# First weights, first residual block and three constants loaded by GpSimd's queue, the second half planned anew, and constant matmuls in TensorE's planned gaps

## The chip, the cores and the metric

The kernel runs on one core of one Trainium2 chip. The core has five instruction streams of its own: TensorE (PE in the profile; its weight loads are PEld), VectorE (DVE), ScalarE (ACT), GpSimd (POOL) and SyncE (SP). Transfers between main memory and the core's SBUF are issued by an instruction of SP, ACT or POOL and carried out by 16 DMA engines beside the compute. The metric is device time of one execution in microseconds (us); lower is better. A comparison gives the median of several executions.

## The reference

Two residual steps over 2048 tokens of 448 channels, each scaled and shifted by rows made of one conditioning vector `c`. The first step is a long convolution along the tokens whose kernel is generated from complex parameters; the second is a gated feed-forward layer with 1792 hidden channels. Everything is float32.

```python
mod = (silu(c) @ w_mod).reshape(1, 6, 1, 448)
sa, ca, ga, sb, cb, gb = (mod[:, i] for i in range(6))
h = layernorm(x) * (1 + ca) + sa
x = x + ga * A(h)
h = layernorm(x) * (1 + cb) + sb
x = x + gb * B(h)

def A(u):                                   # D = 448, N = 256, L = 2048
    K = einsum("dn,dnl,dn->dl", C, exp(dt * A_ * arange(L)), dt * B_).real
    return irfft(rfft(pad(u)) * rfft(pad(K)))[:L] + u * Dskip

def B(x):
    return (gelu(x @ w_gate) * (x @ w_up)) @ w_down
```

## The kernel before

**Two halves.** The first half (to about 400 us of the profile) normalizes the input, generates the convolution kernel and convolves. Six rows of `w_mod` are multiplied with `silu(c)` on TensorE (`mod_row`, task `m.mm`, the multiplications at L768); three of them are needed first, since they scale the first normalization (`norm`, L822 and L823). The normalized input goes through a small transform on TensorE (`ua`, L832) and is stored for later. In parallel the parameters are prepared on VectorE and ScalarE (`prep`), stored, and read back as `lt`; from `lt` come exponentials (`x.mm`, `y.mm`, L593 and L612) and angles (L630) on TensorE, which ScalarE evaluates, VectorE multiplies (L679 to L687) and TensorE contracts (`kgen`, L710). Transforms and products (`k_fft`, then `t_fft` for the last 128 channels: forward L1069, products L1075 and L1078 on VectorE, inverse L1085 on TensorE, eviction `t.z`, store `t.st` L1093) end the half.

**The junction.** The convolution's result is stored to main memory and read back as `yi` (`yi.e` for the first 320 channels; `yi.l0`, `yi.l1` and the short `yi.d..` for the last 128, issued by SP, POOL and ACT, L1154 and L1166). `conv_out(0)` multiplies `yi` with a constant `ai` (L1246 for columns 0 to 320, L1251 for the rest), adds it to the first block of the input, `x1` (L1257), takes the statistics (L1258, L1260, L1274), normalizes (`co.n`, L1288 and L1289), transposes on TensorE with the constant `ident` (`co.t`, L1294 and L1296) and splits the result into two float16 halves `ht` (`co.h` on either engine, `co.l` L1304 on VectorE). For its first two token groups (j = 0, 1) the product is done in two parts, `e` for columns 0 to 320 and `l` for the rest.

**The second half** is the feed-forward layer over four token blocks, the first of them in two halves of 256 tokens for its first four feature groups: `gate_up` (L1365, L1371) and the down product (L1441 for block 0, L1472 after it). Its float32 weights are loaded in pieces of 512 KB (`weight`, L1187, tile `w`, three buffers), split into two float16 parts `wr` (ScalarE L1195, VectorE L1199 and L1200) and stored to main memory for the later blocks.

**What sets the order.** `Plan` holds every piece of work as a `Task` with an engine (or a choice of two), an assumed duration, a due value `v`, and what it depends on. `Plan.order` places the tasks one after the other in the time that it assumes; the due values are shifted by the tables `LEAD` and `LEAN`, numbers per kind of task. What comes out is a fixed list for each engine, which runs in order; real waits are semaphores. SP's list holds nearly all transfers. A transfer takes one of eight completion semaphores in turn, so an issue can also wait for the transfer eight places back. `Plan.run` calls the tasks' functions in the planned order; the tables are long and their numbers tell a reader nothing.

Constants are loaded by `sp`, whose default queue is SP:

```python
def sp(n, v, dst, src, kb, deps=(), alloc=(), use=(), q="SP"):
    qf = adma if q == "ACT" else dma
    return add(n, {q: 0.42 if q == "SP" else 0.1}, v, lambda: qf(dst(), src()), deps, alloc, use, kb=kb)
```

Of the kernel before, what the change touches and what calls it, by code (L numbers as in the profile page):

```python
# [41 lines left out]
    "c.ai": (71.008,), "c.ak": (31.634,), "c.au": (64.741,), "c.ea": (129.571,), "c.id": (-5.74,), "c.ih": (81.5,),  # L42
    "c.ld": (-70.212,), "c.rd": (36.588,), "co.add": (126.534,), "co.adde": (-479.654,), "co.addl": (177.332,),
    "co.addx": (510.429, 276.254, 263.838, 306.027), "co.c2": (-16.462, 185.363, 68.605, 81.504),
    "co.h": (1287.071, 1321.404), "co.h2": (-57.238, -19.565, -34.416, 62.618), "co.l": (166.825, 99.971),
    "co.l2": (-304.102, -376.884, -381.167, -327.959), "co.mm": (1047.13,), "co.mme": (35.95,),
    "co.mml": (321.391,), "co.mmx": (504.891, 504.282, 510.751, 509.801), "co.n": (-32.018, -300.752),
    "co.nx": (-309.183, -245.328, -200.245, -90.738), "co.rc": (52.991, 384.121), "co.rcx": (915.491,),
    "co.rt": (-12.141, 45.958), "co.rtx": (-618.711,), "co.t": (505.324, 339.683),
    "co.t2": (-464.884, -636.939, -578.467, -639.884),  # L50
    "cos": (-96.053, -141.432, -54.911, -135.117, -68.696, -62.333),
# [6 lines left out]
    "dt": (81.074,), "e.f": (-100.312, 117.922), "e.hi": (227.13, 344.995), "e.ld": (-39.805, -1.088),  # L58
    "e.lo": (8.272, -319.182), "ev.end": (-23.435,), "ev.fp": (-187.94,), "ev.geg": (-67.509,), "ev.ub": (109.206,),
    "f.fc": (-74.649, -73.839, -55.611, 15.224, 63.434, 91.147),  # L60
# [6 lines left out]
    "gu": (497.845, 500.786, 503.249, 509.096, 515.626, 545.649),  # L67
    "gu.g": (-625.109, -552.414, -602.197, -714.965, -686.389, -501.12), "gu.h0": (645.72, 522.69),
    "gu.ha": (-729.389, -596.515, -731.42, -528.62, -704.301, -709.342),
    "gu.hs": (-239.586, -121.625, -135.62, -164.459, -9.293, -189.977), "gu.l0": (-16.693, -130.465),  # L70
    "gu.la": (-265.608, -410.165, -336.957, -514.583, -455.359, -305.327),
    "gu.ls": (191.831, 190.571, 255.197, 314.456, 219.503, 228.103),
    "gu.m": (114.811, 93.18, 25.848, 285.848, 134.211, 151.44),
# [22 lines left out]
    "sin2": (46.891, 86.759, 111.859, -3.781, 88.196, 21.274), "t.fc": (52.17, 4.168), "t.fwd": (-57.224, -139.59),  # L96
# [54 lines left out]
class Plan:  # L151
# [106 lines left out]
    def run(self):  # L258
        for t in self.order():
            t.fn(t.on) if len(t.eng) > 1 else t.fn()  # L260
# [89 lines left out]
def s4_geglu(ctx: ExitStack, tc: tile.TileContext, a: dict, out: bass.AP):  # L350
# [342 lines left out]
    KGT = {}  # L693

    def kgen(s, deps):
        m = s // 2
        if s % 2 == 0:
            KG[m] = Buf("kg")

# [423 lines left out]
    def VB(blk):  # L1123
        return 58.5 if blk == 0 else 100.0 + 20.0 * blk - 20.0
# [519 lines left out]
```

## Time and profile before

| what | value |
|---|---|
| median of 3 runs (lowest, highest) | 825.76 us (824.82, 829.9) |
| the profiled execution: its time, its span | 825.18 us, 823.4 us |
| busy in the span: TensorE, VectorE, ScalarE, GpSimd | 748.4, 599.6, 470.3, 6.0 us |
| mean granted TensorE clock | 0.969 of full speed |
| moved by DMA | 136.83 MB, mean 166 GB/s |

The page's strips cut the span into 40 slices of 20.6 us; a digit is the busy share of a slice in tenths. TensorE's strip is at 9 from about 430 us to the end and lower in the first five slices and in the one that begins at about 400 us. The last two strips are the DMA engines' mean share and the rate.

```profile
PE   2786789999799999998589999999999999999997
ACT  5598999899968999971244553034442353113320
DMA  9552369996858846899669756245315322022101
```

In the tables by stage, a row has the stretch, then for each engine its busy time and, in brackets, the number of its instructions, then the granted clock, the DMA engines' share and the rate. In a timeline a row has start, duration, engine, line, operation, output and inputs, the shape and the count of instructions merged into it; where the engine was idle before, the idle time and what ended it stand in square brackets.

### The profile page before, as it was taken

To read this page: it belongs to the slowest core of one execution; us is meant where nothing else is said; L and a number is where in the kernel's file an instruction comes from. 1 tells how busy PE (TensorE), PEld (TensorE's weight loads), DVE (VectorE), ACT (ScalarE), POOL (GpSimd) and SP (SyncE) were. 2 spreads that over 40 slices of the span, in tenths; PEclk is the share of its full clock that TensorE was granted. 3 is DMA by queue.
4 is the path that set the end of the run, shared out by engine and by line. 5 is a ranking of instruction groups with operands and counts; after the bars stand their busy time and mean duration, and the time that the engine had idled before them with its cause. 6 is when DMAs were issued, how large, how long until landed. Compare 5 with 4: busy or idle time off the path is not lost.

```text
span 823.4 us, 19059 instructions
## 1 busy us (share of the span) xinstructions
PE 748.4 (91%) x8166; PEld 461.2 (56%) x8166; DVE 599.6 (73%) x981; ACT 470.3 (57%) x629; POOL 6.0 (1%) x14
## 2 busy tenths in 40 slices
PE   2786789999799999998589999999999999999997
PEld 1344344444577767778466445444496445864477
DVE  7789998999889989897494783178863686244542
ACT  5598999899968999971244553034442353113320
POOL 0000000000000000000200000000000000000000
PEclk9888799999999999999889999999999999999999
DMA  9552369996858846899669756245315322022101
GB/s 283 148 167 92 105 189 236 285 273 200 236 146 257 233 133 193 253 307 295 189 197 298 267 179 179 75 140 166 117 53 146 135 91 90 34 79 90 45 12 35
DMA packets 92526, 136.83 MB, mean 166 GB/s; under 512 B 21280, under 2 KB 75200, under 8 KB 92442
## 3 DMA queue, kind: packets, MB, share of 16 engines
q1 hardware_dynamic: 89514, 133.75, 53.8%
q10 hardware_dynamic: 2608, 1.61, 0.8%
q8 instruction: 64, 1.05, 0.5%
q0 software_dynamic: 320, 0.26, 0.1%
q14 instruction: 20, 0.16, 0.1%
HBM read 100.48 MB, written 36.01 MB: 166 GB/s over the span
## 4 chain that ended last, share of the span: by engine, by line
PE 67%; ACT 12%; DVE 10%; DMA 6%; issue 3%; SPq 1%; DVEq 0%; ACTq 0%
PE pq L1371 30%; PE pq L1472 9%; PE pd L1441 3%; PE kg L710 3%; ACT fg L643 2%; PE pg L630 2%; PE pf L999 2%; PE pq L1365 2%; PE pf L768 2%; ACT my L617 2%; PE pf L1085 2%; PE pf L895 2%; DVE tx L679 2%; DMA fg<-in_w_mod 2%; PE pd L1472 1%
## 5 line engine op out<-in xcount | busy, mean ns | idle before, releaser
L1371 PE MATMUL pq<-ht,wr 128*128 128x512 f16 (+1 forms) x1200 | 250.0, 367 | 0.0
L1371 PEld LDWEIGHTS <-wr 128*128 128x128 f16 x1200 | 115.4, 98 | 128.6 <-issue 11.0
L1378 ACT ACTIVATE ge<-pq 128x512 f32<-128x512 f32 (+1 forms) x60 | 33.9, 568 | 144.5 <-PE pq L1365 93.9
L1385 DVE TENSOR_TENSOR fq<-ge,pq 128x512 f32<-128x512 f32 (+1 forms) x60 | 38.5, 649 | 72.1 <-PE pq L1371 48.2
L1397 ACT ACTIVATE hh<-fq 128x1024 f16<-128x1024 f32 (+1 forms) x49 | 47.1, 963 | 54.5 <-DVE fq L1385 41.8
L1472 PE MATMUL pq<-d,hh 128*128 128x224 f16 x504 | 73.2, 259 | 0.0
L710 PE MATMUL kg<-ty,tx 128*32 128x64 f32 x3584 | 61.8, 221 | 11.3 <-DVE ty L687 6.4
L679 DVE TENSOR_TENSOR tx<-mx,fg 128x1024 f32<-128x1024 f32 x56 | 68.0, 1220 | 4.0 <-ACT fg L654 2.2
L683 DVE TENSOR_TENSOR ty<-my,fg 128x1024 f32<-128x1024 f32 x56 | 68.2, 1219 | 3.0 <-PE kg L710 2.8
L710 PEld LDWEIGHTS kg<-ty,tx 128*32 128x32 f32 x3584 | 53.0, 110 | 27.6 <-issue 11.2
L1472 PE MATMUL pq<-d,hlo 128*128 128x224 f16 x252 | 65.3, 259 | 0.0
L1400 DVE TENSOR_TENSOR hlo<-fq,hh 128x1024 f16<-128x1024 f32 (+1 forms) x49 | 53.9, 1104 | 5.3 <-ACT hh L1397 5.0
L643 ACT ACTIVATE fg<-pg 128x1024 f32<-128x1024 f32 x56 | 56.6, 1019 | 1.9 <-issue 1.2
L1472 PEld LDWEIGHTS <-hh 128*128 128x128 f16 x588 | 56.7, 98 | 1.1 <-issue 0.4
L617 ACT ACTIVATE my<-pg 128x1024 f32<-128x1024 f32 x56 | 55.3, 1041 | 3.1 <-PE pg L612 2.9
L999 PE MATMUL pf<-q,fc 128*128 128x160 f32 x264 | 42.9, 313 | 0.3 <-DVE q L989 0.3
L630 PEld LDWEIGHTS <-lt 64*128 64x128 bf16 x336 | 20.7, 95 | 37.4 <-issue 20.7
L999 PEld LDWEIGHTS pf<-q,fc 128*128 128x128 f32 x264 | 37.7, 195 | 6.3 <-issue 3.3
L630 PE MATMUL pg<-ea,lt 64*128 64x512 bf16 x168 | 34.9, 389 | 6.2 <-ACT fg L643 4.4
L687 DVE TENSOR_TENSOR ty<-my,fg 128x512 f32<-128x512 f32 x56 | 38.4, 686 | 0.0
L686 DVE SCALAR_TENSOR_TENSOR ty<-my,fg 128x512 f32<-128x512 f32 x56 | 38.4, 685 | 0.0
L735 PE MATMUL kg<-ak,ke 128*64 128x128 f32 x448 | 32.1, 284 | 6.2 <-DVE ke L730 4.4
(172 smaller groups left out, 1196.3 us busy)
## 6 DMA issues: line engine op xcount, KB each, us to landing
wr<-w_d SPq DMA_DIRECT2D x21, 896.0 KB
fc<-in_k_fc SPq DMA_DIRECT2D x20, 576.0 KB
u_d<-so SPq DMA_DIRECT2D x32, 224.0 KB
w<-in_wgu SPq DMA_DIRECT2D x14, 512.0 KB
ui<-u_d SPq DMA_DIRECT2D x10, 672.0 KB
w_d<-wr SPq DMA_DIRECT2D x7, 896.0 KB
fq<-in_wd SPq DMA_DIRECT2D x14, 448.0 KB
us<-uo SPq DMA_DIRECT2D x22, 240.0 KB
```

Source lines behind the costliest of these rows:

```text
L617: A.activation(yb.tile.rearrange("p a b c -> p (a b c)"), pb.tile, AF.Exp)
L630: T.matmul(pa[:, nh * 512:nh * 512 + 512], w, x, start=(k == 0), stop=(k == 2))
L643: A.activation(fb.tile[:, 0].rearrange("p x (n k) -> p n x k", n=2), pb.tile.rearrange("p (n x k) -> p n x k", n=2, x=2), AF.Sin, scale=TW ...
L679: V.tensor_mul(tx.tile, xb.tile[:, xm, None, :].to_broadcast([128, 2, 512]), fb.tile[:, :, 0])
L683: V.tensor_mul(ty.tile[:, 1], yb.tile, fy()[:, 1, :, None, :].to_broadcast([128, 16, 2, 32]))
L710: T.matmul(kg[32 * g:32 * g + 32, 2 * (s % 2) + q, :64], tx[:, r, nh, 4 * q + g], ty[:, r, nh, 4 * q + g], start=(r == 0 and nh == 0), sto ...
L999: T.matmul(pz.tile[:, e % 32 - sl0], fc.tile[:, i, 1 + t], pp.tile[:, t, i], start=(t == 0 and e != 32), stop=(t == 1 and e != 0))
L1371: T.matmul(pb[k].tile[:, ts], wr.tile[:, 4 * lo + t, k, c0:c0 + 128], ht[:, m, ts], start=f % 2 == 0 and i == 0, stop=f % 2 == 1 and i == 9)
L1385: V.tensor_mul(to if half is None else to[:, half:half + 1], *src)
L1397: A.activation(hg.tile[0][:, cb, c], fq.tile[:, c], AF.Copy)
L1400: V.tensor_sub(hg.tile[1][:, cb, c], fq.tile[:, c], hg.tile[0][:, cb, c])
L1472: T.matmul(bank(k)[:, m], x[:, p, q[0], ts], w[:, p, q[1]], start=new and m == 0 and p == 0 and z == 0, skip_group_check=True, stop=i in ( ...
```

## The change

Three edits and the tables that follow from them.

1. Loads change their queue. The three constants of the second half (`ai`, `ident`, `idenh`), the first residual block `x1`, and the weights of the first three column groups (`w`, six loads) are issued by GpSimd. The first column group's two loads no longer wait for a store of the transforms (`hold`).
2. `Plan.run` notes for each TensorE task how long TensorE stands idle before it in the planned time, and `spin` issues that many multiplications of a constant (the layernorm epsilon, spread over 128 x 128 and 128 x w by a stride of zero, float32) into the PSUM tile that the task is about to write. The count is the idle time less 1.2, divided by 0.4 for 448 columns and in proportion for fewer. Their results are overwritten.
3. The tables `LEAD` and `LEAN` have new numbers for the second half, the tail of the transforms and the constants.

```diff
@@ tables: some 90 of the rows change @@
-    "c.ai": (71.008,), "c.ak": (31.634,), "c.au": (64.741,), "c.ea": (129.571,), "c.id": (-5.74,), "c.ih": (81.5,),
+    "c.ai": (-45.617,), "c.ak": (24.994,), "c.au": (41.949,), "c.ea": (33.018,), "c.id": (41.212,),
...
@@ Plan.run @@
+        free = 0.0
         for t in self.order():
+            if t.on == "PE":
+                t.idle, free = t.start - free, t.start + t.eng["PE"]
             t.fn(t.on) if len(t.eng) > 1 else t.fn()
...
+    def spin(me, dst, w=D):
+        for _ in range(int(max(0.0, me[0].idle - 1.2) / (0.4 * w / D))):
+            T.matmul(dst, eps.to_broadcast([128, 128]), eps.to_broadcast([128, w]), start=True, stop=True)
+
     def sp(n, v, dst, src, kb, deps=(), alloc=(), use=(), q="SP"):
-        qf = adma if q == "ACT" else dma
-        return add(n, {q: 0.42 if q == "SP" else 0.1}, v, lambda: qf(dst(), src()), deps, alloc, use, kb=kb)
+        qf = {"ACT": adma, "SP": dma, "POOL": P.dma_start}[q]
+        return add(n, {q: 0.42 if q == "SP" else 0.6}, v, lambda: qf(dst(), src()), deps, alloc, use, kb=kb)
...
@@ mod_row; the same two lines stand in x.mm, kgen, ua, conv_out and its transposes @@
         def mm():
             pb.tile = fft.tile([128, D], FT, name="pf")
+            spin(me, pb.tile)
...
@@ conv_out @@
+                    spin(me, pb.tile[:, c0:c1], c1 - c0)
...
@@ x1_load @@
-            dma(xb.tile, a["A_u"][blk])
-        return add("x1.ld", {"SP": 0.42}, VB(blk) - 5, go, deps, [xb], kb=918)
+            (dma if blk else P.dma_start)(xb.tile, a["A_u"][blk])
+        return add("x1.ld" if blk else "x1.lp", {"SP": 0.42} if blk else {"POOL": 0.6}, VB(blk) - 5, go, deps, [xb], kb=918)
...
@@ weight @@
-            dma(wb.tile, a["wgu"][cb, :, k])
+            (P.dma_start if cb < PRE else dma)(wb.tile, a["wgu"][cb, :, k])
         gate = EV["end"] if cb < PRE else CO[0][1]
-        hold = [YO[2, 2]] if cb < 1 else YL
-        t1 = add("w.ld", {"SP": 0.42}, v - 3, ld, [EV["end"]] + hold, [wb], kb=540)
+        hold = [] if cb < 1 else YL
+        t1 = add("w.ld" if cb >= PRE else "w.lp", {"SP": 0.42} if cb >= PRE else {"POOL": 0.6}, v - 3, ld, [EV["end"]] + hold, [wb], kb=540)
...
-    c_ai = sp("c.ai", 58, lambda: K2["ai"], lambda: a["k_ai"], 32, [EV["end"]])
+    c_ai = sp("c.ai", 58, lambda: K2["ai"], lambda: a["k_ai"], 32, [EV["end"]], q="POOL")
...
```

What this does to the engines' lists: on every compute engine the list is the same as before, but for the constant matmuls, up to the tail of the transforms (TensorE's first other difference is some 1676 rows down). On SP, four early constant loads change places. The constant matmuls stand at three places only: 33 and 7 at the start, 61 at the junction.

**TensorE at the start.** `pf<-fg,pk` are the three rows of `w_mod` that are needed first, `pf<-xt,au` the first transform of the input, `lt` the parameters read back; `small` is the tile that holds the constant. Before:

```order
L768 MATMUL pf_178<-fg_122,pk_101 128x448 x4
L768 MATMUL pf_188<-fg_124,pk_101 128x448 x4
L768 MATMUL pf_203<-fg_126,pk_101 128x448 x4
L832 MATMUL pf_243<-xt_118,au_107 128x448
L832 MATMUL pf_244<-xt_118,au_107 128x448
L612 LDWEIGHTS lt_224
L612 MATMUL pg_249<-ea_104,lt_224 128x512
```

and after:

```order
L418 MATMUL pf_178<-small_72 128x448 x33
L785 MATMUL pf_178<-fg_122,pk_101 128x448 x4
L785 MATMUL pf_221<-fg_124,pk_101 128x448 x4
L785 MATMUL pf_236<-fg_126,pk_101 128x448 x4
L418 MATMUL pf_276<-small_72 128x448 x7
L853 MATMUL pf_276<-xt_118,au_107 128x448
L853 MATMUL pf_277<-xt_118,au_107 128x448
L624 LDWEIGHTS lt_257
L624 MATMUL pg_289<-ea_104,lt_257 128x512
```

33 constant matmuls of 448 columns now stand ahead of the first real work, and 7 between the rows of `w_mod` and the transform of the input.

**TensorE at the junction**, with buffer numbers, from the last inverse transforms (`pf<-q,..`) to the `l` parts of the first block (`pd<-yi,ai`, 128 columns). Before:

```order
L1085 MATMUL pf_5325<-q_5266,fg_5122 128x128 x4
L1085 MATMUL pf_5325<-q_5266,my_4941 128x128 x4
L1085 MATMUL pf_5343<-q_5298,my_5015 128x128 x4
L1085 MATMUL pf_5343<-q_5298,my_5045 128x128 x4
L1085 MATMUL pf_5357<-q_5318,my_5120 128x128 x2
L1246 MATMUL pd_5362<-yi_5166,ai_5149 64x320 x2
L1246 MATMUL pd_5367<-yi_5166,ai_5149 64x320 x2
L1251 MATMUL pd_5362<-yi_5166,ai_5149 64x128 x2
L1251 MATMUL pd_5367<-yi_5166,ai_5149 64x128 x2
```

and after:

```order
L1107 MATMUL pf_5353<-q_5345,my_5124 128x128 x4
L1271 MATMUL pd_5366<-yi_5227,ai_5189 64x320 x2
L1271 MATMUL pd_5374<-yi_5227,ai_5189 64x320 x2
L1107 MATMUL pf_5382<-q_5305,fg_5085 128x128 x2
L1107 MATMUL pf_5382<-q_5305,fg_5160 128x128 x6
L1107 MATMUL pf_5401<-q_5316,fg_5160 128x128 x4
L1107 MATMUL pf_5401<-q_5316,my_4981 128x128 x4
L1107 MATMUL pf_5415<-q_5350,my_5162 128x128 x2
L418 MATMUL pd_5366<-small_72 128x128 x61
L1276 MATMUL pd_5366<-yi_5227,ai_5189 64x128 x2
L1276 MATMUL pd_5374<-yi_5227,ai_5189 64x128 x2
```

The `e` parts moved ahead of the last three inverses, and 61 constant matmuls of 128 columns stand between the last inverse and the `l` parts.

**VectorE at the junction.** The first weights' split (`wr<-w,wr`) stood behind the `e` parts' additions (`x1<-x1,pd`); now it stands among the products of the transforms (`q<-my,pf`). After:

```order
L1097 TENSOR_TENSOR q_5305<-my_4742,pf_5278 128x512
L1221 SCALAR_TENSOR_TENSOR wr_5293<-w_5206,wr_5293 128x3x256
L1222 SCALAR_TENSOR_TENSOR wr_5293<-w_5206,wr_5293 64x256
L1097 TENSOR_TENSOR q_5316<-my_4809,pf_5286 128x512
L1100 TENSOR_TENSOR q_5274<-my_4742,pf_5242 64x512
L1221 SCALAR_TENSOR_TENSOR wr_5293<-w_5208,wr_5293 128x3x256
L1222 SCALAR_TENSOR_TENSOR wr_5293<-w_5208,wr_5293 64x256
```

and a little further down the additions and the last four evictions (`lh`, `zo`), which were ScalarE's:

```order
L1097 TENSOR_TENSOR q_5350<-my_4936,pf_5332 128x128
L1100 TENSOR_TENSOR q_5350<-my_4936,pf_5332 64x128 x2
L1100 TENSOR_TENSOR q_5305<-my_4742,pf_5278 64x512 x2
L1100 TENSOR_TENSOR q_5316<-my_4809,pf_5286 64x512 x2
L1282 TENSOR_TENSOR x1_5219<-x1_5219,pd_5366 128x320
L1283 BN_STATS st2_5377<-x1_5219 128x6
L414 COPY lh_5392<-pf_5353 128x512
L1282 TENSOR_TENSOR x1_5219<-x1_5219,pd_5374 128x320
L1283 BN_STATS st2_5377<-x1_5219 128x6
L414 COPY lh_5411<-pf_5382 128x512
L414 COPY zo_5420<-pf_5401 128x512
L414 COPY zo_5422<-pf_5415 128x128
```

Both splits moved ahead of the last products. The eviction of `pf_5382` stands behind both additions, and the inverse into `pf_5415` needs that PSUM buffer, since inverses have two.

**GpSimd's list**, whose only transfers before were eight of `yi<-y` (the last 128 channels) and two of `yi<-zo`. After, its first transfers are:

```order
L1209 DMA w_5206<-in_wgu 128x1024
L1209 DMA w_5208<-in_wgu 128x1024
L422 DMA ai_5189<-in_k_ai 128x64
L1142 DMA x1_5219<-in_A_u 128x1792
L422 DMA ident_5190<-in_k_id 128x128
L422 DMA idenh_5191<-in_k_ih 128x128
L1176 DMA yi_5227<-y2_69 6x2x512
```

Six loads are ahead of the `yi` transfers, and four more `w` loads follow behind them.

More of the change, by code (lines that the diff above doesn't have):

```diff
@@ L712, in go @@
                                      tile_position=(0, 32 * g))
[L713 to L714 removed]
+        me.append(add("kgen", {"PE": 1.04}, s, go, list(deps) + [KGT.get(s - 1) if s % 2 else None],
+                      [KG[m]] if s % 2 == 0 else [], [TX[s], TY[s]] + ([KG[m]] if s % 2 else [])))
+        return me[0]
     AKB = [Buf("ak%d" % (g % 2)) for g in range(3)]
```

88 lines of the change are left out of this document (48 added, 40 removed), and 21 rows, old and new, of tables (LEAD, LEAN).

## The prediction

> **What bounds the kernel now.** I read the table by stage first, to see which engine is full where. Columns: stretch and its length, busy time (instructions) of each engine, granted clock, DMA share, rate.
>
> ```profile
> span 823.4 us, 19059 instructions
> 0.00:15.90 15.90, 0.00 (x0) 0.00 (x0) 10.25 (x32) 11.14 (x18) 0.20 (x4) 1.00 0.91 280
> 15.90:28.30 12.40, 12.26 (x24) 5.72 (x24) 8.10 (x20) 4.17 (x9) 0.00 (x0) 1.00 0.62 179
> 28.30:50.00 21.70, 15.45 (x60) 7.46 (x61) 19.38 (x39) 15.97 (x22) 0.00 (x0) 0.69 0.68 174
> 100.00:376.00 276.00, 256.28 (x4683) 167.44 (x4671) 251.45 (x359) 248.83 (x317) 0.00 (x0) 0.99 0.78 229
> 376.00:400.20 24.20, 23.66 (x206) 22.74 (x206) 17.72 (x28) 6.81 (x12) 3.44 (x6) 1.00 0.91 246
> 400.20:410.20 10.00, 0.04 (x2) 0.00 (x1) 4.08 (x8) 2.00 (x2) 2.33 (x5) 0.70 0.50 159
> 421.50:426.00 4.50, 4.50 (x29) 3.05 (x28) 4.44 (x8) 1.04 (x3) 0.00 (x0) 0.64 0.36 117
> 426.00:818.00 392.00, 391.85 (x2543) 229.03 (x2542) 225.84 (x387) 130.94 (x183) 0.00 (x0) 1.00 0.38 121
> ```
>
> TensorE works 391.85 of the 392.00 us after 426 at full clock, on the same matmuls as afterwards: the new plan has nothing to win there. From 100 to 376 three engines are each 90% to 93% busy and hand work to one another, so that stretch starts as late as its input comes. Only two places have TensorE idle for long: the start and the junction at 400 us. The constant matmuls stand at just these.
>
> Then the chain of waits at the start (start, length, what):
>
> ```profile
> 2.63 13.19 DMA fg<-in_w_mod
> 15.96 12.27 PE pf L768 x24
> 28.33 4.86 DMA lt<-lh_d
> 33.24 1.39 PE pg L612 x4
> 34.63 1.49 PE pf L832 x4
> 36.55 2.22 PE pf L832 x4
> 43.72 1.70 PE pf L832 x4
> 45.44 5.77 DMA xt<-in_A_u
> ```
>
> The kernel waits for the first row of `w_mod`, multiplies until 28.23, and only then can ScalarE (whose list has the third row's eviction ahead of the `lt` loads) fetch `lt`. Everything later hangs on this chain: a delay of these multiplications is a delay of the whole first half.
>
> **The price of one constant matmul.** No row shows one, but the multiplications at L768 have the same type and width: 12 in the program, 24 records, so each is two passes. TensorE's weight loads mark the passes, and VectorE's first row is the constant's fill:
>
> ```profile
> 0.81 0.06 DVE L371 MEMSET small<- 128x1 f32 x1 [0.81 <-PEq L1632]
> 19.82 0.34 PEld L768 LDWEIGHTS pf<-fg,pk 112*128 112x128 f32 x1 [0.41 <-issue]
> 20.57 0.34 PEld L768 LDWEIGHTS pf<-fg,pk 112*128 112x128 f32 x1 [0.41 <-issue]
> 22.41 0.19 PEld L768 LDWEIGHTS pf<-fg,pk 112*128 112x128 f32 x1 [0.19 <-issue]
> 22.79 0.19 PEld L768 LDWEIGHTS pf<-fg,pk 112*128 112x128 f32 x1 [0.19 <-issue]
> 31.48 1.16 PE L832 MATMUL pf<-xt,au 64*128 64x448 f32 x4 [3.26 <-issue]
> ```
>
> A pass takes 0.75 us cold (19.82 to 20.57) and 0.375 us warm; 8 cold ones make 6.0 us, 16 warm ones 6.0 us, which is nearly the 12.27 of the chain. A warm matmul is thus 0.75 us. The plan divides its idle time by 0.4: the constant matmuls last almost twice as long as the gap they are to fill.
>
> **Term 1, the start: +9.0 us.** 33 matmuls are 66 passes from about 1.0 us on. All warm they are 24.75 us; with 8 cold ones, as the row shows after idleness, 27.75 us, and that I take, so they end at 28.8 instead of leaving TensorE free at 15.96. The real 24 passes follow warm, 9.0 us, to 37.8: 9.6 later than 28.23. Seven more constants take 14 passes, 5.25 us, to 43.0. The transform of the input was ready 3.26 us after the rows (the bracket at 31.48), at 41.1, so it waits 1.9 more and starts 11.5 us late; `lt`, issued 9.6 late, lands at 42.8 and finds TensorE busy too. Against this, TensorE now arrives warm. In the chain between 28.3 and 45.4 its four pieces above last 6.8 us at a clock of 0.69; what a full clock can save there is bounded by half, 3.4, and by nothing; I take 2.5. Net +9.0; the ends are +5 (all 66 passes warm, 3.4 saved) and +11.5 (nothing saved).
>
> A rule bears on the cold part. The Trainium skill (TensorE: Matmul & The Clock Gate, Part 1) says that the clock is released after about 3.4 us of sustained work; the row shows 6.0 us. By the rule some 4 or 5 passes are cold, and this term would be 1.3 us smaller.
>
> It passes on: up to the tail of the transforms each engine's list is unchanged, and the pieces of the chain between are issued by work that is itself late. The early loads that change places on SP stand behind the three `w_mod` loads and have until 43 us: nothing.
>
> **Term 2, the junction: +3.5 us.** The rows of TensorE, then of VectorE:
>
> ```profile
> 392.82 3.07 PE L1085 MATMUL pf<-q,fg 128*128 128x128 f32 x26
> 395.72 3.29 PE L1085 MATMUL pf<-q,my 128*128 128x128 f32 x28
> 398.94 1.30 PE L1246 MATMUL pd<-yi,ai 128*64 128x320 f32 x8
> 410.23 1.32 PE L1251 MATMUL pd<-yi,ai 128*64 128x128 f32 x8 [9.99 <-DMA yi<-y]
> 420.25 0.94 PE L1294 MATMUL pq<-ident,xn 128*128 128x128 f32 x6 [3.07 <-DVE xn L1289]
> 421.54 3.92 PE L1371 MATMUL pq<-ht,wr 128*128 128x256 f16 x20
> 425.72 2.36 PE L1371 MATMUL pq<-ht,wr 128*128 128x256 f16 x20
> ```
>
> ```profile
> 400.68 0.47 DVE L1257 TENSOR_TENSOR x<-x,pd 128x320 f32<-128x320 f32 x1
> 401.19 0.49 DVE L1258 BATCH_NORM_STATS2 st<-x 128x6 f32<-128x320 f32 x1
> 403.83 0.96 DVE L1199 SCALAR_TENSOR_TENSOR wr<-w,wr 128x768 f16<-128x768 f32 x1
> 404.71 0.41 DVE L1200 SCALAR_TENSOR_TENSOR wr<-w,wr 64x256 f16<-64x256 f32 x1
> 416.77 0.59 DVE L1257 TENSOR_TENSOR x<-x,pd 128x448 f32<-128x448 f32 x1
> 417.40 0.63 DVE L1258 BATCH_NORM_STATS2 st<-x 128x6 f32<-128x448 f32 x1
> 418.80 0.67 DVE L1288 SCALAR_TENSOR_TENSOR xn<-x,mv,rows 128x448 f32<-128x448 f32 x1
> 419.50 0.69 DVE L1289 SCALAR_TENSOR_TENSOR xn<-xn,rs,rows 128x448 f32<-128x448 f32 x1
> 421.52 0.69 DVE L1304 TENSOR_TENSOR ht<-pq,ht 128x512 f16<-128x512 f32 x1
> ```
>
> Times here are without term 1. *When the last inverse ends.* VectorE gets the two first weights' splits ahead of the last products, 2 x (0.96 + 0.41) = 2.7 us, then the two additions of 0.96, between which it evicts. The last inverse waits for the second eviction; TensorE had little slack here (28 passes left at 395.72), so I let the last inverse end at 402.5 where inverses and `e` parts ended at 400.2; ends 400.2 and 403. *The constants.* A warm pass of 128 columns is 0.118 us (3.07 / 26). 61 matmuls are 122 passes, 14.4 us, and they wait for nothing, so the `l` parts begin at 416.9, not 410.23: +6.7. The `yi` loads, 10 us behind the last work now and relieved of the `w` loads, are hidden. *Won back.* From 410.23 to the end of the second `lo` at 422.2 VectorE's list loses one addition with statistics (1.3) and one normalization with its small step (1.5), which move behind: 12.0 becomes 9.2, then most of a warm multiplication (2.36 less its first four of 20, and 0.4 for L1365): the first feed-forward step ends 11.5 us after the `l` parts begin, at 428.4, where it was 425.7: +2.7. *Given back.* Two transposes instead of one now stand behind the second step; one is 1.3 us (420.25 to 421.54): +4.0. I take 3.5; without the late inverse it would be 1.5, and with nothing won but the cold 1.56 (3.92 to 2.36), 6.7 - 1.6 = 5.
>
> **The queue: 0.** Six of GpSimd's loads go ahead of `yi`. They can be issued when the tables' tiles of the first half come free, about where the stretch from 376.00 begins; the first `yi` issue is at 392.8. One GpSimd issue takes (least, median, most, in ns):
>
> ```profile
> L1154 POOL DMA_DIRECT2D yi<-y x8: 557/564/723, 392.8 to 407.7; - x8
> ```
>
> If a load of 512 KB costs GpSimd as much, six are 3.4 us; even at four times that they are over before `yi`. The bytes are the same and come earlier, into a stretch whose DMA share is 0.91 already; what they push back there is covered by the 14.4 us of constants. If that cover went, the `yi` chain (410.23 before) would be next. SP loses six `w` issues; what those delayed is behind the same cover. *After 426*: the same matmuls, 0.
>
> Sum: 825.2 (the profiled execution, 1.8 outside its span; the median, 825.76, is 0.6 above) + 9.0 + 3.5 = 837.7 us. The terms' ends together make 832 to 842.
>
> **Rivals.**
>
> *The constants are cheap (the other side).* If a constant read with stride zero took one pass, the start's 33 would cost 6.0 cold and 9.4 warm, end at 16.4 and leave warm rows until 25.4: -2.8; and 61 would be 7.2 us and end at 409.7, so the junction keeps what it wins: 0.5 earlier, 2.8 and 1.6 won, 1.3 given back, -3.6. With 1 us of warmth in between: 818 us. It decides where one costs under (15.96 - 1.0) / 33 = 0.45 us. For it: a constant with stride zero brings no new data. Against: 24 records for 12 matmuls, one of whose operands has stride zero already. The Trainium skill (FP8 and Floating Point Precision) says that true float32 takes 4 passes through the array, whatever the values; by that, 448 x 4 columns at the 2.4 GHz that the Trainium skill gives in TensorE: Matmul & The Clock Gate would be an estimated 0.75 us; the trace's 0.75 agrees.
>
> *The delay fades.* If the first half's engines, each idle 7% to 10% of 276 us, make up two thirds of term 1, and the inverses end as before: 825.2 + 3 + 1.5 = 830. Against: their idle time is waiting for one another.
>
> *GpSimd is held up.* Each of the ten `w`, `x1` and constant issues sits behind a VectorE instruction of up to 1 us, `x1` comes late, and the additions hold VectorE's evictions: 837.7 + 5 = 843. The Trainium skill (SBUF — State Buffer, the "DVE blocks DMA" trap) has this as a rule: GpSimd cannot write descriptors while some VectorE copies run. The row above, 557 to 723 ns beside busy products, shows no such wait.
>
> *The constants don't keep the clock up*: then 2.5 and 1.6 us of the sum are not won, 842 us, within the range. Against: the warm passes at 22.41 come after only 6 us of work.
>
> **How the numbers follow.** My forecast 0.74 (its own range 832 to 842), fading 0.14, cheap constants 0.07, GpSimd held up 0.05; the unwon clock is in the first. Range for 8 in 10: 829.5 to 843. About 1%, 8.3 us, is what a measurement of this kernel can tell from no change. Slower (over 834.0): 0.74 less its lower tail of 0.09, and 0.05: 0.70. Faster (under 817.5): half of the cheap case, 0.03. Within 1%: 0.27.
>
> **What would show it.** The 33 constants: about 66 records ending near 29 us; L768 ends near 38; first `lt` matmul at 43 to 44. If they end at 16, the price fails; if L832's first record is 11 late and the stretch at 370 only 3 late, the passing on fails. At the junction 122 records of some 14 us with no gap behind them; a gap there would say that `yi` or GpSimd is late. After it the first L1401 step of 20 in about 2.4 us, and the last matmul some 12 us later than 818.

## The result, and the profile after

| what | before | after |
|---|---|---|
| median (lowest, highest), 4 runs each | 826.12 us (824.82, 829.9) | 836.32 us (835.42, 838.02) |
| ratio of after to before, 95% interval | | 1.0119 [1.0077, 1.016] |
| the profiled execution: its time, its span | 825.18, 823.4 us | 837.15, 835.3 us |
| busy in the span: TensorE, GpSimd | 748.4, 6.0 us | 786.2, 11.3 us |
| mean granted TensorE clock | 0.969 | 0.983 |

The kernel became 1.2% slower, at a higher mean clock. TensorE is busy 37.8 us longer: it has 46.2 us of constants (26.91, 5.45 and 13.79 in the rows below), and its other work takes 8.4 us less.

The timeline of TensorE at the start, after the change (start, duration, engine, line, operation, output and inputs, shapes, count; in brackets the idle time before and what ended it):

```profile
0.92 26.91 PE L418 MATMUL pf<-small 128*128 128x448 f32 x66 [0.92 <-DVE small L393]
27.67 9.18 PE L785 MATMUL pf<-fg,pk 112*128 112x448 f32 x24
36.69 5.45 PE L418 MATMUL pf<-small 128*128 128x448 f32 x14
42.07 1.02 PE L853 MATMUL pf<-xt,au 64*128 64x448 f32 x4
42.93 0.60 PE L624 MATMUL pg<-ea,lt 64*128 64x512 bf16 x4
```

33 constants leave 66 records, two passes each. They end at 27.8; the rows of `w_mod`, which could have begun at about 16 (15.96 before), follow without a gap and end at 36.8 where they ended at 28.2. The first transform of the input begins at 42.07 instead of 31.48.

The same view at the junction, after the change:

```profile
406.90 1.50 PE L1107 MATMUL pf<-q,my 128*128 128x128 f32 x12
408.24 13.79 PE L418 MATMUL pd<-small 128*128 128x128 f32 x122
421.96 0.66 PE L1276 MATMUL pd<-yi,ai 128*64 128x128 f32 x8
425.44 0.94 PE L1323 MATMUL pq<-ident,xn 128*128 128x128 f32 x6 [0.89 <-DVE xn L1315]
429.03 0.60 PE L1401 MATMUL pq<-ht,wr 128*128 128x256 f16 x4 [0.91 <-ACT ht L412]
430.81 3.34 PE L1401 MATMUL pq<-ht,wr 128*128 128x256 f16 x16 [1.19 <-DVE ht L1333]
434.60 2.36 PE L1401 MATMUL pq<-ht,wr 128*128 128x256 f16 x20
439.16 2.36 PE L1401 MATMUL pq<-ht,wr 128*128 128x256 f16 x20
```

The 122 passes run from the last inverse to the `l` parts without a gap behind them: when they end at 422.0, `yi` has landed, though not long ago (the last `yi` load of SP has its last semaphore update at 420.03). The `l` parts are warm (0.66 us for 8, before 1.32), but the first feed-forward step is in two pieces, and its second piece, 16 multiplications, takes 3.34 us where all 20 of the second step take 2.36: cold again.

Since most of each engine's list is the same in both kernels, the same VectorE instruction can be looked up in both timelines. How much later it starts tells where time was lost and where it came back:

| VectorE instruction | before | after | later by |
|---|---|---|---|
| statistics of the input | 51.23 | 60.20 | 8.97 |
| `lh` from `q` | 102.26 | 111.20 | 8.94 |
| `ty` from `my`, `fg` | 151.07 | 162.58 | 11.51 |
| `ty` from `my`, `fg` | 223.85 | 234.78 | 10.93 |
| eviction of `ke` | 241.94 | 249.05 | 7.11 |
| `ty` from `my`, `fg` | 354.36 | 361.43 | 7.07 |
| `q` from `my`, `pf`, in the tail | 379.93 | 386.02 | 6.09 |
| `fq`, first feed-forward group | 432.07 | 442.18 | 10.11 |
| `xn` in block 0's down product | 511.56 | 522.54 | 10.98 |
| the last `xn` | 818.65 | 830.21 | 11.56 |

The start costs 9.0 us, as forecast, and the junction 4.0. But the delay did not simply pass on between them: it grew by 2.5 us, then lost 3.8 between 224 and 242 and 1.0 between 354 and 380, and after the junction 1.45 came on top.

The loss of 3.8 us has a row. The timeline of TensorE before the change, two contractions of 64 records each, and further down one of 16:

```profile
221.67 1.88 PE L710 MATMUL kg<-ty,tx 128*32 128x64 f32 x107
226.93 0.86 PE L710 MATMUL kg<-ty,tx 128*32 128x64 f32 x21 [3.38 <-issue]
227.71 3.11 PE L999 MATMUL pf<-q,fc 128*128 128x160 f32 x12
...
362.34 0.93 PE L735 MATMUL kg<-ak,ke 128*64 128x128 f32 x13 [1.51 <-issue]
```

TensorE stops for 3.38 us in the middle of the second one, after 43 of its 64 records, and waits for no engine and no transfer of the program that the profile shows. The twelve passes behind it (L999) take 3.11 us; after the change the same twelve take 1.90, so the stop also costs 1.2 us of cold clock. The last row has a shorter stop of the same kind. After the change there is no such stop: from 45 us on the longest wait put down to "issue" is 0.92 us, at 239.64.

### The profile page after: what moved, and what is told of

It reads as the page before. It is cut to its first block, busy times and chain, and to the rows that moved or that the text cites. A ratio compares the mean times of both kernels' runs of the same rounds, so it can differ in the third digit from the quotient of the medians.

```text
span 835.3 us, 19489 instructions
## 1 busy us (share of the span) xinstructions
PE 786.2 (94%) x8368; PEld 486.2 (58%) x8368; DVE 599.9 (72%) x983; ACT 470.2 (56%) x627; POOL 11.3 (1%) x24
## 4 chain that ended last, share of the span: by engine, by line
PE 59%; ACT 9%; DVE 6%; issue 3%; DMA 2%; SPq 0%; DVEq 0%; ACTq 0%
PE pq L1401 29%; PE pq L1502 9%; PE pd L1471 4%; ACT fg L655 2%; PE pq L1395 2%; ACT fg L647 2%; PE kg L723 2%; PE pd L418 2%; PE pf L1021 2%; PE pd L1502 1%; PE pg L642 1%; ACT fg L659 1%; PE pf L917 1%; PE pd L1271 1%; PE pf L1008 1%
```

## The experiments

Each was timed beside the kernel before on its own chip; the ratios are to that.

| kernel | median us | ratio, 95% interval |
|---|---|---|
| after, no constants | 831.16 | 1.0042 [1.0017, 1.0067] |
| after, half the constants | 821.96 | 0.9944 [0.9903, 0.9985] |
| after, constants at the start only | 836.59 | 1.0103 [1.0066, 1.0139] |
| after, constants at the junction only | 832.9 | 1.0073 [1.0048, 1.0097] |
| after, 40 tiny ones at the start, no others | 824.74 | 0.9961 [0.994, 0.9983] |
| before, with 16 and 3 at the start | 815.75 | 0.9878 [0.9844, 0.9913] |
| after, half the constants, loads on SP | 820.05 | 0.993 [0.9899, 0.9961] |
| before, with 16 and 3, and 38 at the junction | 819.94 | 0.992 [0.9891, 0.9948] |
| before, 40 tiny ones at the start | 824.8 | 0.9968 [0.9941, 0.9994] |
| before, with 16 and 3, and 21 tiny ones | 819.54 | 0.9927 [0.9901, 0.9954] |
| before, with 16 and 3, and 13 in a gap | 815.85 | 0.9887 [0.9849, 0.9924] |
| after, 16 and 3, none at the junction, loads on SP | 822.29 | 0.9946 [0.9915, 0.9978] |

The kernel before was at a median of 826.75 (first four), 827.42 (next four) and 828.38 us (last four), with single runs from 819 to 837.

**1. No constants.**

```diff
-        for _ in range(int(max(0.0, me[0].idle - 1.2) / (0.4 * w / D))):
+        for _ in range(0):
```

> No constant matmuls at all; queues, plan and lists as in the changed kernel. My theory (the constants cost the time, since each is two passes and twice as long as planned): the start is as before, 28.2 us for the end of the first rows of w_mod; the l parts begin when yi lands, near 410, cold; one addition and one normalization less ahead of the first feed-forward step, one transpose given back: about 824 us, 821 to 828. Rival 1 (the new plan or the queue is what costs): 830 or more. Rival 2 (the constants help and only something else hurts): no faster than the changed kernel, 836.

831.16 us: a miss. Taking every constant away gives back 5.2 of the 10.2 us, not all. By its ratio, the queue and the plan alone cost 3.5 us (1.4 to 5.5). The stop inside the contraction is there again, at the same place, 42 of 64 records in. Its timeline of TensorE:

```profile
228.95 0.54 PE L723 MATMUL kg<-ty,tx 128*32 128x64 f32 x22 [3.63 <-issue]
404.65 1.50 PE L1107 MATMUL pf<-q,my 128*128 128x128 f32 x12
417.38 1.32 PE L1276 MATMUL pd<-yi,ai 128*64 128x128 f32 x8 [11.22 <-DMA w<-in_wgu]
```

The last inverse ends at 406.15 and the `l` parts begin 11.2 us later, as in the kernel before (399.01 to 410.23, with the `e` parts between). The bracket names a `w` load, but the `l` parts need `yi`, and the last `yi` load of SP (issued at 411.51) still updated its semaphore at 416.82. So the junction, which was to win a little without constants, wins nothing: VectorE was 3.8 us late ahead of the junction (377.81 before, 381.58 now), and its row of the first feed-forward group is 4.3 late behind it (432.07, 436.40).

Most of the loss thus lies ahead of the junction, where every compute engine's list is that of the kernel before: VectorE is 1.5 us late at 129, 2.6 at 151, 2.1 at 242 and 3.8 at 378. That GpSimd's queue or the new second half cause this part is not shown.

**2. Half the constants.**

```diff
-        for _ in range(int(max(0.0, me[0].idle - 1.2) / (0.4 * w / D))):
+        for _ in range(int(max(0.0, me[0].idle - 1.2) / (0.8 * w / D))):
```

> Half as many constants: the count is divided by 0.8 for 448 columns, the measured price, so 16 and 3 at the start and 30 at the junction. My theory: 16 end near 14 us, ahead of the first row of w_mod, and the 24 real passes then run warm in 9.0, so the rows end near 25 (28.2 before); at the junction 60 passes are 6.8 us and end about when yi lands; the feed-forward steps then start warm: about 820 us, 816 to 824. Rival 1 (the new plan or the queue costs): 830 or more. Rival 2 (the clock does not carry over into the real work): no better than the kernel without constants.

821.96 us, within the expected range, 14.4 us under the changed kernel. The timeline of TensorE, the start and the junction:

```profile
16.06 9.26 PE L785 MATMUL pf<-fg,pk 112*128 112x448 f32 x24 [0.97 <-DMA fg<-in_w_mod]
28.53 1.02 PE L853 MATMUL pf<-xt,au 64*128 64x448 f32 x4 [0.95 <-DVE xt L841]
394.76 6.86 PE L418 MATMUL pd<-small 128*128 128x128 f32 x60
407.26 1.32 PE L1276 MATMUL pd<-yi,ai 128*64 128x128 f32 x8 [5.64 <-DMA yi<-y]
```

At the start all is as intended: TensorE waits 0.97 us for the row of `w_mod` as before, and the 24 passes take 9.26 us instead of 12.26, so that they end at 25.3 where they ended at 28.2. At the junction the 30 constants end 5.6 us too early; the `l` parts begin cold (1.32) and 12.3 us after the last inverse.

**3 and 4. The start alone, and the junction alone.**

```diff
-        for _ in range(int(max(0.0, me[0].idle - 1.2) / (0.4 * w / D))):
+        for _ in range(int(max(0.0, me[0].idle - 1.2) / (0.4 * w / D)) if w == D else 0):
```

```diff
-        for _ in range(int(max(0.0, me[0].idle - 1.2) / (0.4 * w / D))):
+        for _ in range(int(max(0.0, me[0].idle - 1.2) / (0.4 * w / D)) if w < D else 0):
```

> Only the 33 and 7 at the start, none at the junction. My theory: the start is 9.0 us late as in the changed kernel, some 3 of it is won back on the way to the tail, and the junction is that of the kernel without constants: about 830 us, 827 to 834. Rival (the start's delay is made up and the junction's 61 cost all): within 2 us of the kernel without constants.

> Only the 61 at the junction, none at the start. My theory: the 122 passes of 0.113 us hold the l parts some 5 us past the landing of yi, and a part of it comes back as a warm first feed-forward step: 3 to 6 us over the kernel without constants, about 829 us, 826 to 832. Rival (the junction's constants are hidden behind yi): equal to the kernel without constants or faster by the warm step.

836.59 and 832.9 us. Against the kernel without constants the start's 40 cost 5.4 us and the junction's 61 cost 1.7, which the scatter of these runs hardly tells from nothing; both together (the changed kernel) cost 5.2. Both times are above the ranges that I gave (834 and 832), because the kernel without constants is itself 7 us above what I expected of it; the junction's 1.7 is less than the 3 to 6 that I expected over that kernel. The profiles say why the start's price is not 9: with its constants the stop of 3.4 us is away, with the junction's alone it is there, in the timeline of TensorE of the fourth kernel:

```profile
229.04 0.86 PE L723 MATMUL kg<-ty,tx 128*32 128x64 f32 x22 [3.36 <-issue]
407.66 13.79 PE L418 MATMUL pd<-small 128*128 128x128 f32 x122
```

**5. 40 tiny ones at the start.** The same count of instructions at the same two places, 32 x 16 instead of 128 x 448; none at the junction.

```diff
-            T.matmul(dst, eps.to_broadcast([128, 128]), eps.to_broadcast([128, w]), start=True, stop=True)
+            T.matmul(dst[:32, :16], eps.to_broadcast([128, 32]), eps.to_broadcast([128, 16]), start=True, stop=True)
```

> As the kernel without constants, but the 33 and 7 constants at the start stand in the list as 32 x 16 multiplications, which take next to no time; none at the junction. The clock should be cold at the first rows of w_mod, and nothing there earlier or later than without constants. It separates two readings of TensorE's stall of 3.4 us inside a contraction at 227 to 229 us, which the kernels without start constants have and those with them have not. Theory A (it hangs on where in TensorE's instruction stream the place lies): the stall is gone as in the changed kernel, and the time is 3 to 5 us under the kernel without constants, about 827 us. Theory B (it hangs on when TensorE comes there): the stall stays, 831 us.

824.74 us, 6.4 under the kernel without constants, more than the 3 to 5 expected: at 220 us, ahead of the stop, VectorE is already 2.3 us earlier than there. Its timeline of TensorE:

```profile
0.92 3.70 PE L418 MATMUL pf<-small 128*32 128x16 f32 x66 [0.92 <-DVE small L393]
17.26 12.13 PE L785 MATMUL pf<-fg,pk 112*128 112x448 f32 x24 [12.63 <-DMA fg<-in_w_mod]
223.26 1.90 PE L1021 MATMUL pf<-q,fc 128*128 128x160 f32 x12
```

The rows of `w_mod` are as cold as before (12.13 us), and VectorE is half a microsecond late up to 129 us (129.08 before, 129.59 now), so nothing was won at the start. The stop is gone, and the twelve passes behind it are warm (1.90 us, before 3.11): VectorE's lead goes from 0.5 us at 220 (220.22, 219.72) to 5.6 at 239 (238.86, 233.24), some 4.6 of it from these two. What decides on the stop is where TensorE's list stands, not when TensorE gets there: theory A.

**6. The old plan with 16 and 3 at the start.**

```diff
+    N1, N2 = [16], [3]
...
             pb.tile = fft.tile([128, D], FT, name="pf")
+            spin(pb.tile, N1.pop() if N1 else 0)
...
                     pbs[h].tile = fft.tile([128, D], FT, name="pf")
+                spin(pbs[0].tile, N2.pop() if N2 else 0)
```

> The kernel before, with its queues and its plan, and 16 and 3 constants at the start only. My theory: the rows of w_mod end 3 us earlier as in the kernel with half the constants, the stall of 3.4 us at 227 goes too, and the old plan keeps the 3 to 4 us that the new plan and the queue cost: 818 to 821 us. Rival (the new plan is worth something once the constants are sized right): 822 us or more, no better than the kernel with half the constants.

815.75 us, 1.2% under the kernel before and the best of all: better than forecast. Its timeline of TensorE:

```profile
0.92 14.37 PE L414 MATMUL pf<-small 128*128 128x448 f32 x32 [0.92 <-DVE small L389]
15.13 9.18 PE L775 MATMUL pf<-fg,pk 112*128 112x448 f32 x24
221.63 1.08 PE L716 MATMUL kg<-ty,tx 128*32 128x64 f32 x59 [1.00 <-issue]
404.58 1.32 PE L1259 MATMUL pd<-yi,ai 128*64 128x128 f32 x8 [9.89 <-DMA yi<-y]
416.79 2.96 PE L1379 MATMUL pq<-ht,wr 128*128 128x256 f16 x20
```

The start wins 3 to 4 us (VectorE is 4.0 early at 102), the longest stop left is 1.00, and the junction is that of before. VectorE's lead grows by 3.7 us between 224 and 242, where the stop was. The profiled execution was the slowest of the four, 819.08 us; where the faster ones won the rest is not shown.

**7. Half the constants, the loads on SP.** The compute engines' lists are those of experiment 2, word for word.

```diff
-        qf = {"ACT": adma, "SP": dma, "POOL": P.dma_start}[q]
+        qf = {"ACT": adma, "SP": dma, "POOL": dma}[q]
...
-            (dma if blk else P.dma_start)(xb.tile, a["A_u"][blk])
+            dma(xb.tile, a["A_u"][blk])
...
-            (P.dma_start if cb < PRE else dma)(wb.tile, a["wgu"][cb, :, k])
+            dma(wb.tile, a["wgu"][cb, :, k])
```

> The kernel with half the constants, and the ten loads issued by SP at the places that the new plan gives them, instead of GpSimd; all compute lists are the same. My theory: with GpSimd the two w loads of 512 KB start beside the last yi loads, and the l parts wait for yi until 12.4 us after the last inverse, where it was 10.0; with SP they start behind the yi loads: the l parts begin 2 to 4 us earlier and the time is 1 to 4 us shorter, about 819.5 us. Rival (the queue costs nothing, the plan alone is at fault): 822 us, within 1 us of the kernel with half the constants. Second rival (the queue helps): 824 us or more.

820.05 us, 1.9 under experiment 2; the two intervals overlap, so the time alone doesn't settle it. The place does. Its timeline of TensorE, and below it GpSimd's in experiment 2:

```profile
393.70 6.86 PE L418 MATMUL pd<-small 128*128 128x128 f32 x60
403.75 1.35 PE L1276 MATMUL pd<-yi,ai 128*64 128x128 f32 x8 [3.19 <-DMA yi<-y]
```

```profile
398.90 0.55 POOL L1176 DMA_DIRECT2D yi<-y  x1 [0.45 <-issue]
399.44 1.15 POOL L1209 DMA_DIRECT2D w<-in_wgu  x2
```

From the end of the last inverse to the `l` parts there are now 9.9 us, where experiment 2 has 12.3 and experiment 1 has 11.2. (The 10.0 of the kernel before, to which I compared in the expectation, is counted from the end of its `e` parts; from its last inverse it is 11.2.) GpSimd issues two `w` loads right behind its last `yi` load, while SP is still issuing three; on SP they stand behind those. The last of the three, issued at 401.21 here, has its last semaphore update in the trace at 403.62; in experiment 2, issued at 400.41, at 406.71. The queue costs 1.3 to 2.4 us there when nothing covers it.

**8. The old plan with 16 and 3, and 38 at the junction.**

```diff
+                    spin(pb.tile[:, c0:c1], 38 if blk == j == 0 and i else 0, c1 - c0)
```

> The kernel before with 16 and 3 constants at the start and 38 of 128 columns ahead of the l parts, sized at 0.226 us each to end 8.6 us after the last inverse, 1.4 us before yi lands. My theory: the l parts and the transposes run warm and the first feed-forward step, which follows a wait of 3 us, stays partly cold: 1 to 3 us under the kernel with the start's constants alone, 816 to 819 us. Rival (the waits of 3 us behind it take the clock away again, so that the warm part shortens nothing that VectorE does not bound): equal within 1 us.

819.94 us, 4.2 above experiment 6 where I had it 1 to 3 below. Its timeline of TensorE:

```profile
392.45 8.75 PE L414 MATMUL pd<-small 128*128 128x128 f32 x76
403.18 0.88 PE L1260 MATMUL pd<-yi,ai 128*64 128x128 f32 x8 [1.98 <-DMA yi<-y]
412.96 1.65 PE L1303 MATMUL pq<-ident,xn 128*128 128x128 f32 x6 [3.43 <-DVE xn L1298]
415.17 4.42 PE L1380 MATMUL pq<-ht,wr 128*128 128x256 f16 x20
```

The `l` parts are warm, but they only wait for VectorE sooner, and the first step is colder (4.42 us) than without the constants (2.96). From the `l` parts to the second step it is 16.7 us here (to 419.85), 15.4 in experiment 6 (to 420.00). That is 1.3 of the 4.2 us; the rest I have not placed. Constants ahead of the `l` parts win nothing.

**9. The old plan with 40 tiny ones at the start.** Experiment 6's edit, with 33 and 7 of 32 x 16.

> The kernel before, its plan and its queues, with 33 and 7 multiplications of 32 x 16 at the start that take 4.3 us in all, in time that TensorE waits anyway. Theory A (the place in TensorE's instruction stream decides on the stalls inside contractions, whatever the plan): the stalls at 227 and 362 us are gone and the time is 4 to 6 us under the kernel before, about 821.5 us. Theory B (the gain was peculiar to the new plan, or the tiny constants do something for the clock at the start): 826 us, or with rows of w_mod at full clock from the start.

824.8 us, 0.3% under the kernel before (0.1% to 0.6%), between the two theories by its time. Its profile has no "issue" wait over 0.64 us, and VectorE's delay goes from 4.6 us at 207 (207.12, 211.70) to a lead of 0.8 at 249 (249.17, 248.41): theory A. What hides the gain is another place, which lost 5 us before it (below).

**10. Experiment 6 with 21 tiny ones.**

```diff
+        for _ in range(n and (17 if n > 3 else 4)):
+            T.matmul(dst[:32, :16], eps.to_broadcast([128, 32]), eps.to_broadcast([128, 16]), start=True, stop=True)
```

> The kernel before with 16 and 3 constants at the start as in the best run so far, and 17 and 4 tiny ones behind them, so that TensorE's stream is moved by 40 instructions instead of 19. Theory A (place in the stream): the last stall of 1.0 us at 221 is gone too: 0.5 to 1.5 us under 815.75, about 814.7. Rival (19 are as good as 40): 815.75 within 0.7.

819.54 us: a miss for both theories, 3.8 above experiment 6. The longest "issue" wait is 0.50, as A had it, but its rows of `w_mod` begin at 16.8, behind the tiny ones, where they began at 15.1 in experiment 6, and between 106 and 146 us VectorE loses 4.8 (a lead of 3.6 at 105.52, a delay of 1.2 at 145.87).

That stretch is the read-back of the transformed input (`ui<-u_d`, which the first L895 matmuls read, at 128.8 before). From profile to profile it cost 0 to 5 us against the kernel before: about 0 in experiments 5, 7, 8 and 12, 1.2 to 3.2 in the changed kernel and in 1 to 4, 6 and 11, and 4.8 in 9 and 10. No edit of mine sorts these. I leave it open, whether they differ between executions or between programs.

**11. Experiment 6 with 13 in the gap ahead of the third transposes.**

```diff
+                spin(pt.tile[:, 0], 13 if blk == 0 and j == 2 else 0, 128)
```

> The kernel before with 16 and 3 constants at the start, and 13 of 128 columns, 2.9 us, ahead of the third pair of transposes, where TensorE waits 3.43 us for VectorE; none ahead of the l parts. My reading of the clock: it falls when the waits since the l parts sum up to some 3 us within 7, and with the gap filled the third transposes take 0.9 and 0.4 instead of 1.64 and 0.69 and the first feed-forward step 2.36 instead of 2.96: 1 to 1.6 us under 815.75, about 814.4. Rival (the step is bound by VectorE's halves of ht, not by TensorE's clock): equal within 0.7.

815.85 us, equal to experiment 6. Its timeline of TensorE:

```profile
407.98 1.32 PE L1259 MATMUL pd<-yi,ai 128*64 128x128 f32 x8 [10.93 <-DMA yi<-y]
415.19 3.17 PE L414 MATMUL pq<-small 128*128 128x128 f32 x26
418.20 0.83 PE L1303 MATMUL pq<-ident,xn 128*128 128x128 f32 x6
419.33 2.58 PE L1380 MATMUL pq<-ht,wr 128*128 128x256 f16 x20
```

The clock did as I read it: the third transposes take 0.83 and the first step 2.58. From the `l` parts to the second step (422.17) it is 14.2 us instead of 15.4. The time doesn't show these 1.2 us, with runs from 814.0 to 822.2; a gain of that size was not measured.

**12. The new plan, 16 and 3 at the start, no constants at the junction, loads on SP.** Experiment 7 with the condition of experiment 3.

> The new plan with all loads on SP, 16 and 3 constants at the start, none at the junction. It differs from the best run so far by the plan alone. My theory: the plan loses 1.15 us at two waits for the third weights' split near 440 to 460, loses 2.4 us with the last inverse behind two splits on VectorE, and wins some 3 us between the l parts and the first feed-forward steps: 816 to 819 us. Rival (the junction's 30 constants helped): 821 us or more.

822.29 us: by its number the rival's case. But experiment 7, with the junction's 30, is 2.2 faster with an overlapping interval, and its 30 ended 3.2 us before `yi` landed and left the `l` parts cold (1.35), so that they helped is not shown. The new plan is 6.5 us above the old one with the same start (experiment 6; 5.6 by the two ratios), more than the 0 to 3 that I had worked out. The place says that most of this is the second half: from 386 us of the kernel before to the last `xn`, VectorE loses 4.0 us on it here, and 1.4 to 4.2 in experiments 1, 2, 5 and 7, where the old plan's experiments 6, 9 and 10, without constants at the junction, lose nothing (0 to 0.8 won). Its profile has the two waits for the third weights' split at their largest, 2.14 and 0.50 us, at 440.

## Why the prediction was right, and where it was not

- **The price** was right: two passes a constant, 0.375 us each when warm. 33 of them end 11.9 us after the first row of `w_mod` could have begun. Against the rival that constants are cheap stands the row of 66.
- **The cold part** was mis-sized for this run. I took eight cold passes, 6.0 us; the weight loads of the changed kernel show five:

```profile
4.07 0.34 PEld L418 LDWEIGHTS pf<-small 128*128 128x128 f32 x1 [0.41 <-issue]
4.63 0.19 PEld L418 LDWEIGHTS pf<-small 128*128 128x128 f32 x1 [0.22 <-issue]
5.01 0.19 PEld L418 LDWEIGHTS pf<-small 128*128 128x128 f32 x1 [0.19 <-issue]
```

  The spacing falls from 0.75 to 0.38 us at 4.6, 3.7 us after the first pass. The 3.4 us of the Trainium skill (TensorE: Matmul & The Clock Gate, Part 1), which I set against my row, is nearer, and so the constants end at 27.8, not 28.8. The Trainium skill says there too that its window runs freely, so that the number of cold passes depends on where the work falls in it; the runs agree: 6.1 us in the kernels before and without constants, 5.4 with the junction's alone, 3.7 here. In experiment 3, whose first 33 constants are the same, it is 6.2 us: they end at 29.2, and VectorE is 10.5 us late at 51 us instead of 9.0.
- **Term 1, +9.0**, came out at 8.97 by 51 us, by luck, from two errors that cancel: the transform began 10.6 late, not 11.5, and 1.6 was won back, not 2.5.
- **"It passes on"** is the step that failed. 9.0 became 6.1 by the tail. The rival of the fading delay had the direction but not the reason: no engine's slack took it up. The stop of 3.38 us, with the cold passes behind it, was in the kernel before and hangs on the place in TensorE's list, which 40 more instructions moved; experiments 5 and 9 show it without any constant's cost or warmth. (The 1.0 us between 354 and 380, where the kernel before has its stop of 1.51, is less clear: experiment 5 lacks that stop too and loses 0.8 us there.) I had quoted no row of it: in a stretch that I called full by its sum, I did not ask what its 20 idle microseconds were. The 2.5 us lost at the read-back went the other way.
- **Term 2, +3.5**, measured 4.0. The last inverse ended at 408.4, or 402.3 without the shift of 6.1 (I had 402.5); the passes took 13.8, not 14.4; the `l` parts began 5.6 late, not 6.7. Little of that was the constants' own: in experiment 3, which has none here, the `l` parts begin 12.2 us after the last inverse, and here 13.6. The rest is the later inverse and the later `yi`. Too much was counted as won back: the first step was to be warm and was cold. The second transpose's 1.3 was 1.2 (8.9 late at 434.60, 10.1 at 439.16).
- **The queue at 0**: right in the changed kernel by the cover that I named, but only just: `yi` landed some 2 us before the constants ended, where I had 6.7. Experiments 2 and 7 show that it holds the `l` parts back by 2.4 us once the cover is short, so not all of the +3.5 goes with the constants. GpSimd held up by VectorE was not seen: its ten moved issues took 0.53 to 0.66 us each.
- **After 426, 0**: failed by 1.45 us. "The new plan has nothing to win there" was right, but it can lose. In the changed kernel's timeline of TensorE:

```profile
456.35 0.82 PE L1401 MATMUL pq<-ht,wr 128*128 128x512 f16 x3 [0.46 <-ACT wr L1217]
457.86 1.68 PE L1401 MATMUL pq<-ht,wr 128*128 128x512 f16 x7 [0.69 <-DVE wr L1222]
```

  These two waits for the split of later weights, 1.15 us, stand in experiments 1, 2 and 5 with the same lengths, whatever their constants, and not in the kernel before.

So 12.5 us were forecast and 12.0 came between the profiled executions (10.2 between the medians), as 9.0 - 2.9 + 4.0 + 1.45 and 0.4 at the end, where I had 9.0 + 0 + 3.5 + 0. That the sums agree so closely is luck: the 2.9 us that came back ahead of the junction and the 2.4 us that were lost beyond the forecast there and behind it nearly cancel. And the price is not one of the constants alone: with none the changed kernel is still 3.5 us above the kernel before. Sized at half, at the start of the old plan, they go with a gain of 10 us, of which the trace gives some 4 to the warm start and 3.7 to the place of the stop, which nearly free instructions move as well.

## What to carry to other kernels

Work put in to keep an engine's clock up must be priced by a measured row of the same type and width and end before the input of the real work lands: here 16 constants at the start won some 4 us where 33 lost 9, from one wrong divisor. Filler ahead of short dependent work that then waits for another engine buys nothing; it belongs into the last gap ahead of dense work, if anywhere. Before crediting a gain or a loss to an edit that adds instructions, compare it with a control that adds as many nearly free ones, and look for stops inside bursts that wait for nothing.

## What was not expected of the hardware

A burst of TensorE can stop for 3.4 us in its middle, and 19 or 40 instructions two hundred microseconds earlier take that away. The three kernels without added instructions at the start (before, experiments 1 and 4) stop for 3.38, 3.63 and 3.36 us after 42 or 43 of 64 records of the same contraction; the eleven with them have no "issue" wait above 1.00 us after the first 45 us. The Trainium skill (Runtime: NRT & Kernel Launch, Instruction fetch mechanics) says that an engine's instructions are streamed in blocks of 256 and that crossing a block's edge is mostly hidden. The traces bear out both. The page of the kernel before has a queue of the kind "instruction" (packets, MB, share):

```profile
q8 instruction: 64, 1.05, 0.5%
```

These are 64 packets of 16,384 bytes, as many as TensorE's 16,408 records make blocks of 256. I number all of TensorE's records (multiplications, weight loads, semaphore instructions) from 0 in the order of their start. In the fourteen kernels TensorE has 33 waits put down to "issue" that are above 0.1 us and later than 45 us. All 33 stand at a number that leaves 193 to 195 when divided by 256, and all end 1.2 to 1.7 us after such a packet has ended. The packet ended at 225.54, 227.56 and 227.73 us in the kernels with the three long stops, and the contraction went on at 226.93, 228.95 and 229.04. Some 850 other block edges show no such wait. So the burst stops because its next instructions arrive late. Added instructions ahead move the edges to other places; why a packet starts late at one edge and not at another is not shown.

The clock falls without any long wait. In the table by stage of the changed kernel (busy TensorE, PEld, VectorE, ScalarE and GpSimd, then the granted clock), and below it in that of the kernel without constants:

```profile
424.00:431.00 7.00, 3.94 (x34) 2.72 (x31) 6.82 (x15) 2.62 (x5) 0.42 (x1) 1.00 0.00 0
431.00:434.70 3.70, 3.70 (x21) 2.18 (x20) 3.56 (x9) 1.83 (x3) 0.11 (x1) 0.54 0.42 146
```

```profile
421.00:427.00 6.00, 3.95 (x34) 2.82 (x31) 5.85 (x12) 1.53 (x4) 0.53 (x1) 1.00 0.00 0
427.00:431.00 4.00, 4.00 (x39) 3.24 (x37) 3.86 (x10) 2.37 (x4) 0.00 (x0) 1.00 0.38 131
```

After waits that sum to 3.1 us in 7, none of them over 1.2, the clock is at about half for the first step; after 2.05 us in 6 it stays. Fourteen microseconds of dense constants just ahead did not prevent it. The granted clock does not tell everything: for 15.90 to 28.30 us of the kernel before it reads 1.00, while the first passes there take 0.75 us and the later ones 0.375, so at the start the spacing of the passes has to be read instead.
